# Whole batches first, mixed tiles last, opening masks on TensorE and a new opening order, in an attention and feed-forward kernel

## The chip, the cores and the metric

The kernel runs on one core of one Trainium2 chip. The metric is the device time of one launch in microseconds (us); lower is better.

A profile is one execution. Its span is about 1.7 us shorter than the device time of the same run. Engines: PE is TensorE's matmuls and PEld its weight loads, DVE is VectorE, ACT is ScalarE, POOL is GpSimd, SP is SyncE, which here issues all DMAs.

## The reference

Eight batches of 576 tokens, 8 heads of 64. Each token attends to itself and the 63 tokens before it in its batch; then every token goes through a gated feed-forward block.

```python
def _attn_ref(q, k, v):
    B, H, S, D = q.shape                  # 8, 8, 576, 64
    window = 64
    scores = np.matmul(q, k.transpose(0, 1, 3, 2)) / np.sqrt(D)
    rel = np.arange(S)[:, None] - np.arange(S)[None, :]
    scores = np.where((rel >= 0) & (rel < window), scores, -1e9)
    attn = softmax(scores)
    return np.matmul(attn, v)

def _moe_ref(x, w_gate, w_val, w_out):    # x: 4608 x 512, d_ff 1536
    g = x @ w_gate
    return (g * sigmoid(g) * (x @ w_val)) @ w_out
```

## The kernel before

Tokens are cut into 36 groups of 128, four groups to a feed-forward tile of 512. A batch has 576 = 4.5 x 128 tokens, so every second batch boundary falls in the middle of a group. `load` cuts its DMA there, and one of three masks is chosen for the group. Names: `load(n)` brings keys or queries of 256 tokens (0.52 MB), `load_vg(g)` the values of one group (0.26 MB), `weights(s, i)` a 512 x 256 tile of the gate (0) or value (1) weights (0.52 MB); `turn2` transposes on TensorE, `turn1` through DMA; `step(t, m)` is one of 12 feed-forward steps of a tile (8 matmuls of 512 columns and a tanh), `finish` its VectorE half; `project` is the output matmul; `warm(n)` is n filler matmuls on zeros.

```python
def keys_before(n):                      # last 64 keys of the tile before
    if n:
        dve.tensor_copy(kT[n % KR][:, :, 0:64], kT[(n - 1) % KR][:, :, 256:320])

def weigh(g):                            # exp on ScalarE, mask on VectorE
    E = Es[g % ER]
    mk = masks[0]
    for b in range(2):
        if (2 * g + b) % 9 == 0:
            mk = masks[1 + b]
    for a, x in enumerate(sps.pop(g)):
        e = E[:, a:H:2]
        act.activation(e, x[:], AF.Exp, scale=0.125)
        dve.tensor_mul(e, e, mk[:].unsqueeze(1).to_broadcast([P, 4, 2, 64]))

# the opening, a hand-set order (cut: every "..." leaves lines out)
load(0, k, "k_f"); load(0, q, "q_f")
...
warm(4); scores(0); cast_v(0, (pool, act, dve)); cast_k(1, "k_f", pool)
load(1, q, "q_f"); scores(1); load_vg(2); load(2, k, "k_f"); ...
load(2, q, "q_f") ... load(3, k, "k_f") ... load(3, q, "q_f") ... load_vg(4)
norm(2); products(3); norm(3); cast_k(3, "k_f", pool); weigh(5); turn_x(1); scores(4)
weights(3, 0); cast_k(3, "q_f", pool); weigh(4) ... weights(3, 1)
warm(2); products(4); norm(4); cast_w(3, 1, dve); scores(6); ... step(0, 7)
...
# the regular loop, two groups a turn (cut)
for w in range(8, NG, 2):
    step(t, 3 * s); finish(); ...; scores(w + 4); scores(w + 5); finish(); ...
    turn1(n + 4, "k_f"); keys_before(n + 4); project(t - 1, s); ...
```

The softmax here doesn't subtract the row's maximum and nothing guards it: scores larger than these inputs give would overflow.

## Time and profile before

The device time was 342.47 us, the median of 3 runs (341.31 to 343.25).

| part of the profiled execution (span 342.5 us) | us | read from |
|---|---|---|
| first feed-forward matmul | 31.2 | timeline of TensorE |
| start of the regular loop | 94.3 | timeline of TensorE |
| loop and tail | 248.2 | the rest |
| TensorE busy, 40 to 330 us | 99% | sums by stretch |

The page of before. Each digit is the busy share, in tenths, of one fortieth of the span (8.6 us); PEclk is the clock granted to TensorE, in tenths.

```profile
span 342.5 us, 7053 instructions
...
PE   7677999999999999999999999999999999999996
...
DVE  3869887998577676767676867676777766655520
...
PEclk9968999999999999999999999999999999999999
DMA  8999999997988798979988888898988420200012
...
PE 89%; DMA 4%; DVE 2%; ACT 1%; SPq 1%; issue 1%; ACTq 0%
```

From the fifth slice on TensorE is full, at full clock. Only the first four slices can be shortened; there DMA is 80 to 90% busy or more, VectorE 60 to 90% from the second slice on, and the clock falls. The sums by stretch, with columns PE, PEld, DVE, ACT, POOL (busy us and instructions), clock, DMA share and GB/s:

```profile
10.00:20.00 10.00, 7.11 (x106) 3.99 (x103) 8.46 (x22) 6.99 (x12) 2.38 (x3) 0.89 1.26 227
20.00:30.00 10.00, 6.58 (x111) 4.90 (x113) 7.77 (x21) 7.36 (x13) 6.52 (x8) 0.77 1.11 273
30.00:40.00 10.00, 8.96 (x103) 4.67 (x105) 8.91 (x19) 6.72 (x12) 6.92 (x9) 0.83 1.05 298
```

The chain of waits in the opening (followed back from the last instruction, at each step to what released it), with start and length in us:

```profile
12.90 7.79 DMA q_f<-in_q_dram
...
25.76 2.59 DVE E L191 x4
...
30.95 0.34 PE s_ps L176 x16
31.29 1.65 PE g_ps L269 x4
32.93 1.28 PE v_ps L269 x3
```

It runs through a load of queries that lands at 20.7 us, then through four mask products on VectorE, then into the first step (g_ps), whose matmuls take 0.41 us each: that is the half clock. In the loop they take 0.216 us.

The timeline of TensorE, with start, length, line, operation, shapes and count, gives the first step and the first of the loop:

```profile
31.22 1.72 PE L269 MATMUL g_ps<-xT,wg 128*128 128x512 bf16 x4
...
94.27 1.03 PE L269 MATMUL g_ps<-xT,wg 128*128 128x512 bf16 x4
```

### The profile page before, as it was taken

Reading aid. Unit: us, or ns where it says so; the run is one execution under the profiler, and the core shown is the slowest. Engines: PE = TensorE matmul, PEld = TensorE weight load, DVE = VectorE, ACT = ScalarE, POOL = GpSimd, SP = SyncE. Lnnn points to the kernel's source line nnn. Section 1 sums busy time; section 2 is a strip of 40 time slices with the busy share of each in tenths; the row PEclk is TensorE's granted clock in tenths of the full one; section 3 lists DMA queues with packets and bytes.
Section 4 is the critical chain, followed back from the end, with each engine's and each line's share of the span. In section 5 each row is a group of like instructions: output and inputs, shape, how many; then the busy total and the mean of one; then the engine's idle time right before and its main releaser. Section 6 shows DMA issues by size and latency. Waiting matters only on the chain.

```text
span 342.5 us, 7053 instructions
## 1 busy us (share of the span) xinstructions
PE 327.1 (95%) x2636; PEld 160.9 (47%) x2677; DVE 237.3 (69%) x496; ACT 150.4 (44%) x260; POOL 103.1 (30%) x143
## 2 busy tenths in 40 slices
PE   7677999999999999999999999999999999999996
PEld 3443545455544444444444444444444445444444
DVE  3869887998577676767676867676777766655520
ACT  4756746854362525252525252525343434323222
POOL 2245734552153333332433333333333220000000
PEclk9968999999999999999999999999999999999999
DMA  8999999997988798979988888898988420200012
GB/s 201 236 244 293 322 198 256 352 246 133 181 160 180 167 174 170 171 174 159 186 158 186 155 186 152 190 162 178 179 170 176 110 71 33 62 33 31 31 63 92
DMA packets 148994, 56.70 MB, mean 166 GB/s; under 512 B 122080, under 2 KB 142944, under 8 KB 148960
## 3 DMA queue, kind: packets, MB, share of 16 engines
q1 hardware_dynamic: 148960, 56.25, 77.1%
q8 instruction: 21, 0.34, 0.5%
q14 instruction: 13, 0.11, 0.1%
HBM read 37.75 MB, written 9.44 MB: 138 GB/s over the span
## 4 chain that ended last, share of the span: by engine, by line
PE 89%; DMA 4%; DVE 2%; ACT 1%; SPq 1%; issue 1%; ACTq 0%
PE g_ps L269 28%; PE v_ps L269 27%; PE o_ps L288 26%; DMA q_f<-in_q_dram 4%; PE ao_ps L205 3%; PE s_ps L176 3%; PE tp L147 1%; SPq L81 1%; DVE E L191 1%; DMA out_dram<-os__4803 1%; PE xtp L229 0%; DVE ve L162 0%; ACT q_fb L107 0%; SPq L101 0%; ACT kT L107 0%
## 5 line engine op out<-in xcount | busy, mean ns | idle before, releaser
L280 DVE SCALAR_TENSOR_TENSOR sg<-th,g_ps 128x512 f32<-128x512 f32 (+2 forms) x110 | 74.0, 673 | 56.2 <-ACT th L274 55.9
L269 PE MATMUL g_ps<-xT,wg 128*128 128x512 bf16 (+1 forms) x411 | 110.7, 378 | 2.2 <-DVE sg L280 0.5
L269 PE MATMUL v_ps<-xT,wv 128*128 128x512 bf16 (+2 forms) x435 | 111.0, 377 | 0.1
L274 ACT ACTIVATE th<-g_ps 128x512 f32<-128x512 f32 (+2 forms) x110 | 64.8, 590 | 79.4 <-PE g_ps L269 76.6
L288 PE MATMUL o_ps<-wo,hT 128*128 128x512 bf16 (+2 forms) x453 | 98.5, 368 | 0.2
L281 DVE TENSOR_TENSOR hT<-sg,v_ps 128x512 bf16<-128x512 f32 (+2 forms) x110 | 74.5, 677 | 11.6 <-remote 0.4
L269 PEld LDWEIGHTS <-wv 128*128 128x128 bf16 x440 | 43.0, 98 | 51.2 <-issue 0.5
L288 PEld LDWEIGHTS <-hT 128*128 128x128 bf16 x456 | 43.5, 98 | 49.2
L269 PEld LDWEIGHTS <-wg 128*128 128x128 bf16 x440 | 40.1, 98 | 44.4 <-issue 1.1
L190 ACT ACTIVATE E<-s_ps 128x512 bf16<-128x512 f32 x72 | 38.9, 596 | 12.4 <-PE s_ps L176 12.4
L109 POOL CAST q_fb<-q_f 128x1024 bf16<-128x1024 f32 (+1 forms) x17 | 17.1, 1007 | 87.0 <-DMA q_f<-in_q_dram 85.8
L191 DVE TENSOR_TENSOR E<-E,mask 128x512 bf16<-128x512 bf16 x72 | 34.1, 502 | 9.4 <-ACT E L190 8.6
L109 POOL CAST ve<-v_f 64x512 bf16<-64x512 f32 x57 | 35.6, 625 | 5.2 <-DMA v_f<-in_v_dram 1.7
L109 POOL CAST k_fb<-k_f 128x1024 bf16<-128x1024 f32 (+1 forms) x16 | 15.8, 991 | 56.3 <-DMA k_f<-in_k_dram 45.5
L216 DVE TENSOR_TENSOR x_b<-ao_ps,r 128x256 bf16<-128x256 f32 x72 | 30.5, 424 | 2.5
L109 POOL CAST vo<-v_f 128x512 bf16<-128x512 f32 x30 | 18.9, 631 | 15.1 <-DMA v_f<-in_v_dram 14.8
L205 PE MATMUL ao_ps<-ve,E 128*64 128x65 bf16 x288 | 14.2, 200 | 2.7 <-DVE qT L109 1.6
L205 PEld LDWEIGHTS <-E 128*64 128x64 bf16 x576 | 11.7, 114 | 10.7 <-issue 7.8
L205 PE MATMUL ao_ps<-vo,E 128*64 128x65 bf16 x288 | 14.2, 200 | 0.0
L176 PEld LDWEIGHTS <-kT 64*128 64x128 bf16 x576 | 10.1, 96 | 8.4 <-issue 6.6
L176 PE MATMUL s_ps<-qT,kT 64*128 64x64 bf16 x576 | 12.4, 193 | 1.2 <-DVE qT L109 0.7
L215 DVE RECIPROCAL r<-ao_ps 128x4 f32<-128x4 f32 x72 | 12.4, 172 | 0.6 <-PE ao_ps L205 0.5
(83 smaller groups left out, 130.9 us busy)
## 6 DMA issues: line engine op xcount, KB each, us to landing
v_f<-in_v_dram SPq DMA_DIRECT2D x32, 256.0 KB, 4.4
q_f<-in_q_dram SPq DMA_DIRECT2D x22, 256.0 KB, 4.4
k_f<-in_k_dram SPq DMA_DIRECT2D x22, 256.0 KB, 4.1
w_f<-in_moe_w_gate_dram SPq DMA_DIRECT2D x6, 512.0 KB, 6.7
w_f<-in_moe_w_val_dram SPq DMA_DIRECT2D x6, 512.0 KB, 7.0
wo_f<-in_moe_w_out_dram SPq DMA_DIRECT2D x6, 512.0 KB, 7.8
k_f<-in_k_dram SPq DMA_DIRECT2D x4, 512.0 KB, 6.6
q_f<-in_q_dram SPq DMA_DIRECT2D x4, 512.0 KB, 7.2
```

What stands on the lines that cost most here:

```text
L109: eng.tensor_copy(y, x)
L176: nc.tensor.matmul(ps[a][:, p, b], kT[g // 2 % KR][y, p, o:o + P], qT[g // 2 % QR][y, p, o:o + 64], tile_position=(64 * a, 0),)
L190: act.activation(e, x[:], AF.Exp, scale=0.125)
L191: dve.tensor_mul(e, e, mk[:].unsqueeze(1).to_broadcast([P, 4, 2, 64]))
L205: nc.tensor.matmul(o_ps[64 * b:64 * b + 64, i, :], Es[g % ER][:, y, b], z[g % VR][:, y, :], tile_position=(0, 64 * b),)
L215: dve.reciprocal(r[:], o_ps[:, :, D])
L216: dve.tensor_mul(xb[g][:, 256 * h:256 * h + 256].rearrange("r (y d) -> r y d", y=4), o_ps[:, :, 0:D], r[:].unsqueeze(2).to_broadcast([P, 4 ...
L269: nc.tensor.matmul(ps[:, 0:n], w[:, c, P * m:P * m + P], xT[t][:, c, c0:c0 + n], start=(c == 0), stop=(c == 3),)
L274: act.activation(th[:, 0:n], g_ps[:, 0:n], AF.Tanh, scale=0.5)
L280: dve.scalar_tensor_tensor(sg[:, 0:n], th[:, 0:n], 1.0, g_ps[:, 0:n], ALU.add, ALU.mult)
L281: dve.tensor_mul(hT[t][:, m, c0:c0 + n], sg[:, 0:n], v_ps[:, 0:n])
L288: nc.tensor.matmul(o_ps[:, a:b], hT[t][:, c, P * s:P * s + P], wo[:, c, a:b], start=(c == 0), stop=(c == 11),)
```

## The change

The first 512 tokens of a batch become four whole groups, and the last 64 of two batches share a mixed group (four mixed groups in all, the 29th, 30th, 35th and 36th of the order). No early load is cut at a batch's end. The last keys and values of each batch are kept aside (`kL`, `vL`) until its mixed group comes. Six opening groups (0 and 2 to 6) get their mask from TensorE: after each score matmul a second one adds -1e30 where the mask is zero, and their two VectorE products fall away. The opening is a new hand-set order.

```diff
+    ORDER = [(b, i) for b in range(7) for i in range(4)] + [(0, None), (2, None)]
+    ORDER += [(7, i) for i in range(4)] + [(4, None), (6, None)]
 ...
     def keys_before(n):
-        if n:
-            dve.tensor_copy(kT[n % KR][:, :, 0:64], kT[(n - 1) % KR][:, :, 256:320])
+        b, i = ORDER[2 * n - 1]
+        x = kT[(n - 1) % KR][:, :, 256:320]
+        if i == 3:
+            dve.tensor_copy(kL[:, :, b, 0:64], x)
+        elif i == 1:
+            dve.tensor_copy(kT[n % KR][:, :, 0:64], x)
+
+    def keys_last(n):
+        b, i = ORDER[2 * n]
+        if i is None:
+            dve.tensor_copy(kL[:, :, b:b + 4, 64:P], kT[n % KR]...)   # cut
 ...
-    def scores(g):
+    def scores(g, masked=False):
 ...
+                if masked:
+                    for a in range(2):
+                        y = slice(64 * a, 64 * a + 64)
+                        m = minus[1 if ORDER[g][1] == 0 and b == 0 else 0]
+                        nc.tensor.matmul(
+                            ps[a][:, p, b], m[y], identb[y, y], tile_position=(64 * a, 0),
+                            start=False, stop=True,
+                        )
 ...  (weigh: the mask product only where not masked)
# opening: new order (cut)
+    load(0, q, "q_f")
+    load(0, k, "k_f")
+    cast_k(0, "q_f", (act, dve))
+    load(1, k, "k_f")
+    load_vg(0)
+    cast_k(0, "k_f", (act, pool))
+    load_vg(1)
 ...
+    cast_v(1, (dve, None, None))
+    weigh(1)
+    load(2, q, "q_f")
+    weigh(0)
+    warm(6)
+    products(0)
+    load_vg(2)
+    load_vg(3)
+    weights(5, 0)
+    load_vg(4)
 ...
+    weights(5, 1)
+    load_vg(5)
+    turn2(2, "q_f", act)
+    load(3, k, "k_f")
 ...
+    products(4)
+    cast_w(5, 1, pool)
+    cast_v(5, pool)
+    weigh(5)
+    cast_w(5, 0, dve)
+    step(0, 10, 0, 256)
 ...
# loop and end
             keys_before(n + 4)
+            keys_last(n + 4)
-    for s in range(3):
+    for s in (2, 3, 0):
         project(8, s)
```

More of the change, by code (lines that the diff above doesn't have):

```diff
@@ L32 @@
     NG = NTOK // P
-    NB = NTOK // 256
+    ORDER = [(b, i) for b in range(7) for i in range(4)] + [(0, None), (2, None)]
+    ORDER += [(7, i) for i in range(4)] + [(4, None), (6, None)]
     VW = 65
     KR, VR, ER, QR = 3, 5, 3, 3
+    NEG = -1e30
     ctx.enter_context(tc.manual_schedule())
@@ L58 @@
     ve = [cst.tile([P, H, VW], BF16, name=f"ve{i}") for i in range(VR)]
+    kL = cst.tile([P, 4, 8, P], BF16, name="kL")
+    vL = cst.tile([P, 8, H, VW], BF16, name="vL")
     Es = [cst.tile([P, H, 2, 64], BF16, name=f"E{i}") for i in range(ER)]
-    masks = [cst.tile([P, 2, 64], BF16, name=f"mask{i}") for i in range(3)]
+    masks = [cst.tile([P, 2, 64], BF16, name=f"mask{i}") for i in range(2)]
+    minus = [cst.tile([P, P], BF16, name=f"minus{i}") for i in range(2)]
     identb = cst.tile([P, P], BF16, name="identb")
@@ L67, with tokens @@
     staged = {}
-    def segments(lo, n, step):
-        o = 0
-        while o < n:
-            b, s = divmod(lo + o, S)
-            m = min(n - o, S - s)
-            yield o // step, m // step, b, s, m
-            o += m
+    def tokens(g):
+        b, i = ORDER[g]
+        if i is None:
+            return (slice(0, 64), b, 512), (slice(64, P), b + 1, 512)
+        return ((slice(0, P), b, P * i),)
     def load(n, src, nm):
         x_f = stage.tile([P, H, 2, D], FP32, name=nm, tag=nm)
-        for r, m, b, s, t in segments(256 * n, 256, 2):
-            sp.dma_start(
-                x_f[r:r + m].rearrange("r h c d -> r h (c d)"),
-                src[b, :, s:s + t, :].rearrange("h (r c) d -> r h (c d)", c=2),
-            )
+        ((_, b, s),) = tokens(2 * n)
+        sp.dma_start(
+            x_f[:].rearrange("r h c d -> r h (c d)"),
+            src[b, :, s:s + 256, :].rearrange("h (r c) d -> r h (c d)", c=2),
+        )
         staged[nm, n] = x_f[:].rearrange("r h c d -> r c h d")
@@ L90, in load1 @@
         for i in range(2):
-            for r, m, b, s, t in segments(256 * n + P * i, P, 1):
-                sp.dma_start(x_f[r:r + m, i], src[b, :, s:s + t, :].rearrange("h r d -> r h d"))
+            for y, b, s in tokens(2 * n + i):
+                m = y.stop - y.start
+                sp.dma_start(x_f[y, i], src[b, :, s:s + m, :].rearrange("h r d -> r h d"))
         staged[nm, n] = x_f[:]
@@ L98, in load_vg @@
             staged["v_f", g // 2] = stage.tile([P, 2, H, D], FP32, name="v_f", tag="v_f")[:]
-        x_f = staged["v_f", g // 2]
-        for r, m, b, s, t in segments(P * g, P, 1):
-            sp.dma_start(x_f[r:r + m, g % 2], v[b, :, s:s + t, :].rearrange("h r d -> r h d"))
+        for y, b, s in tokens(g):
+            m = y.stop - y.start
+            sp.dma_start(
+                staged["v_f", g // 2][y, g % 2],
+                v[b, :, s:s + m, :].rearrange("h r d -> r h d"))
     words = {}
@@ L122, in keys_before @@
     def keys_before(n):
-        if n:
-            dve.tensor_copy(kT[n % KR][:, :, 0:64], kT[(n - 1) % KR][:, :, 256:320])
+        b, i = ORDER[2 * n - 1]
[6 more added lines that the diff above has]
+        b, i = ORDER[2 * n]
+        if i is None:
+            dve.tensor_copy(
+                kL[:, :, b:b + 4, 64:P],
+                kT[n % KR][:, :, 64:320].rearrange("r p (b x) -> r p b x", b=4))
     def turn1(n, nm):
@@ L153, in cast_v @@
     def cast_v(g, engs):
+        engs = engs if isinstance(engs, tuple) else (engs,) * 3
         x = staged["v_f", g // 2][:, g % 2]
         lo, hi = slice(0, 64), slice(64, P)
-        engs = engs if isinstance(engs, tuple) else (engs,) * 3
+        b, i = ORDER[g]
         z = vo[g % VR]
-        copy(engs[0], z[:, :, 0:D], x)
-        for e, a, b in ((engs[1], ve[g % VR][hi], lo), (engs[2], ve[(g + 1) % VR][lo], hi)):
+        if i is None:
+            to = (vL[hi, b], lo), (vL[hi, b + 1], hi)
+        else:
+            copy(engs[0], z[:, :, 0:D], x)
+            to = (ve[g % VR][hi], lo), (vL[lo, b] if i == 3 else ve[(g + 1) % VR][lo], hi)
+        for e, (y, a) in zip(engs[1:], to):
             if e is None:
-                dve.tensor_copy(a, z[b])
+                dve.tensor_copy(y[:, :, 0:D], z[a][:, :, 0:D])
             else:
-                copy(e, a[:, :, 0:D], x[b])
+                copy(e, y[:, :, 0:D], x[a])
     sps = {}
-    def scores(g):
+    def scores(g, masked=False):
         ps = [ps_a.tile([P, 4, 2, 64], FP32, name="s_ps", tag="a") for _ in range(2)]
@@ L175, in scores @@
                     y = slice(64 * a, 64 * a + 64)
+                    keys = kT[g // 2 % KR][y, p, o:o + P]
+                    if ORDER[g][1] is None:
+                        keys = kL[y, p, ORDER[g][0] + b, :]
                     nc.tensor.matmul(
-                        ps[a][:, p, b], kT[g // 2 % KR][y, p, o:o + P],
-                        qT[g // 2 % QR][y, p, o:o + 64], tile_position=(64 * a, 0),
-                    )
-        sps[g] = ps
+                        ps[a][:, p, b], keys, qT[g // 2 % QR][y, p, o:o + 64],
+                        tile_position=(64 * a, 0), start=True, stop=not masked,
+                    )
+                if masked:
[5 more added lines that the diff above has]
+                            start=False, stop=True,
+                        )
+        sps[g] = ps, masked
     def weigh(g):
         E = Es[g % ER]
-        mk = masks[0]
-        for b in range(2):
-            if (2 * g + b) % 9 == 0:
-                mk = masks[1 + b]
-        for a, x in enumerate(sps.pop(g)):
+        mk = masks[1 if ORDER[g][1] == 0 else 0]
+        ps, masked = sps.pop(g)
+        for a, x in enumerate(ps):
             e = E[:, a:H:2]
             act.activation(e, x[:], AF.Exp, scale=0.125)
-            dve.tensor_mul(e, e, mk[:].unsqueeze(1).to_broadcast([P, 4, 2, 64]))
+            if not masked:
+                dve.tensor_mul(e, e, mk[:].unsqueeze(1).to_broadcast([P, 4, 2, 64]))
     xT = {}
@@ L199, in products @@
         xps[g] = []
+        c, i = ORDER[g]
+        vs = (ve[g % VR], vo[g % VR]) if i is not None else (vL[:, c], vL[:, c + 1])
         for h in range(2):
@@ L203, in products @@
                 y = 4 * h + i
-                for b, z in enumerate((ve, vo)):
+                for b, z in enumerate(vs):
                     nc.tensor.matmul(
-                        o_ps[64 * b:64 * b + 64, i, :], Es[g % ER][:, y, b], z[g % VR][:, y, :],
+                        o_ps[64 * b:64 * b + 64, i, :], Es[g % ER][:, y, b], z[:, y, :],
                         tile_position=(0, 64 * b),
@@ L283, in project @@
     def project(t, s, parts=((0, DM),)):
-        n0 = 512 * t + P * s
         for a, b in parts:
@@ L293, in project @@
             act.activation(os_[:, a:b], o_ps[:, a:b], AF.Copy, scale=0.5)
-            sp.dma_start(out[n0:n0 + P, a:b], os_[:, a:b])
+            for y, c, n0 in tokens(4 * t + s):
+                n0 += S * c
+                sp.dma_start(out[n0:n0 + y.stop - y.start, a:b], os_[y, a:b])
     def warm(n):
@@ L304, in begin @@
         make_identity(nc, identb[:])
-        for mk in masks:
-            dve.memset(mk[:], 1.0)
+        dve.memset(masks[0][:], 1.0)
+        dve.memset(minus[0][:], 0.0)
         pool.affine_select(
@@ L314, in begin @@
         )
-        dve.memset(kT[0][:, :, 0:64], 0.0)
-        dve.memset(ve[0][0:64], 0.0)
+        for a in range(2):
+            y = minus[0][64 * a:64 * a + 64]
+            pool.affine_select(
+                out=y, in_=y, compare_op=ALU.is_ge, fill=NEG,
+                base=64, pattern=[[-1, P]], channel_multiplier=1,
+            )
+            pool.affine_select(
+                out=y, in_=y, compare_op=ALU.is_ge, fill=NEG,
+                base=-1, pattern=[[1, P]], channel_multiplier=-1,
+            )
@@ L317, in begin @@
+        pool.tensor_copy(minus[1][:, 64:P], minus[0][:, 64:P])
+        pool.memset(minus[1][:, 0:64], NEG)
+        pool.tensor_copy(masks[1][:], masks[0][:])
+        pool.memset(masks[1][0:64, 0, :], 0.0)
+        for i in (0, 2):
+            dve.memset(kT[i][:, :, 0:64], 0.0)
+        for i in (0, 4):
+            dve.memset(ve[i][0:64], 0.0)
         for x in vo + ve:
             dve.memset(x[:, :, D:VW], 1.0)
-        for i in (1, 2):
-            dve.tensor_copy(masks[i][:], masks[0][:])
-            dve.memset(masks[i][0:64, i - 1, :], 0.0)
@@ L323 @@
     begin()
+    load(0, q, "q_f")
     load(0, k, "k_f")
-    load(0, q, "q_f")
-    cast_k(0, "k_f", (dve, act))
-    cast_k(0, "q_f", (act, pool))
+    cast_k(0, "q_f", (act, dve))
[3 more added lines that the diff above has]
+    load_vg(1)
     warm(11)
-    turn2(0, "k_f", act)
-    load_vg(0)
-    load(1, k, "k_f")
+    turn2(0, "q_f", (act, dve))
+    warm(4)
+    turn2(0, "k_f", (act, dve))
+    cast_k(1, "k_f", (dve, act))
     warm(3)
-    turn2(0, "q_f", dve)
@@ L334 @@
-    warm(4)
-    scores(0)
-    cast_v(0, (pool, act, dve))
-    cast_k(1, "k_f", pool)
-    load(1, q, "q_f")
-    scores(1)
-    load_vg(2)
-    load(2, k, "k_f")
-    keys_before(1)
-    weigh(0)
-    cast_k(1, "q_f", dve)
-    weigh(1)
-    warm(2)
-    turn2(1, "k_f", act)
-    warm(2)
-    turn2(1, "q_f", (dve, act))
-    load_vg(1)
-    load(2, q, "q_f")
-    products(0)
-    norm(0)
-    scores(3)
-    cast_k(2, "k_f", (dve, pool))
-    weigh(3)
-    warm(1)
-    turn_x(0)
-    scores(2)
@@ L360 @@
-    cast_v(1, (pool, None, None))
-    weigh(2)
-    load_vg(3)
-    turn2(2, "k_f", act)
-    load(3, k, "k_f")
-    cast_k(2, "q_f", (act, pool))
-    cast_v(2, (pool, dve, act))
-    cast_v(3, (act, pool, pool))
-    warm(2)
-    products(1)
-    norm(1)
-    keys_before(2)
-    warm(4)
-    turn2(2, "q_f", (dve, act))
+    scores(1)
+    load(1, q, "q_f")
+    cast_v(0, (dve, pool, pool))
+    scores(0, True)
+    cast_k(1, "q_f", pool)
+    load(2, k, "k_f")
+    cast_v(1, (dve, None, None))
@@ new lines @@
+    weigh(1)
[7 more added lines that the diff above has]
+    load_vg(4)
+    norm(0)
+    keys_before(1)
+    turn2(1, "k_f", (act, dve))
+    warm(4)
+    turn_x(0)
+    turn2(1, "q_f", (act, dve))
+    products(1)
+    warm(1)
+    scores(2, True)
+    cast_k(2, "k_f", pool)
+    norm(1)
+    cast_k(2, "q_f", dve)
+    weigh(2)
+    warm(1)
+    scores(3, True)
+    weigh(3)
+    weights(5, 1)
+    load_vg(5)
+    turn2(2, "q_f", act)
@@ L374 @@
+    load(3, k, "k_f")
+    cast_v(2, (dve, pool, pool))
+    keys_before(2)
+    turn2(2, "k_f", dve)
+    turn_x(1)
+    warm(2)
     products(2)
     load(3, q, "q_f")
+    norm(2)
+    cast_v(3, (act, pool, pool))
     warm(1)
-    scores(5)
-    load_vg(4)
-    norm(2)
+    scores(4, True)
+    weights(0, 0)
+    weigh(4)
     products(3)
     norm(3)
-    cast_k(3, "k_f", pool)
-    weigh(5)
-    turn_x(1)
-    scores(4)
-    weights(3, 0)
-    cast_k(3, "q_f", pool)
-    weigh(4)
-    turn_x(2)
@@ L390 @@
-    cast_v(4, (pool, None, None))
-    cast_w(3, 0, pool)
-    turn2(3, "k_f", act)
-    turn_x(3)
-    keys_before(3)
-    warm(1)
-    turn2(3, "q_f", (act, dve))
-    weights(3, 1)
-    warm(2)
-    products(4)
-    norm(4)
-    cast_w(3, 1, dve)
-    scores(6)
-    load_vg(5)
-    weigh(6)
-    weights(2, 0)
-    step(0, 7)
-    cast_v(5, (act, pool, pool))
-    scores(7)
-    finish()
-    weights(2, 1)
-    weigh(7)
-    cast_w(2, 0, act)
-    cast_w(2, 1, pool)
-    load_vg(6)
-    products(5)
@@ L416 @@
-    load_vg(7)
-    step(0, 6)
-    turn_x(4)
-    norm(5)
-    cast_v(6, (act, pool, pool))
-    finish()
-    step(0, 5)
-    turn_x(5)
-    finish()
-    weights(1, 0)
-    cast_v(7, (pool, pool, act))
-    weights(1, 1)
-    cast_w(1, 0, pool)
-    products(6)
-    step(0, 4)
-    weights(5, 0)
-    weights(5, 1)
-    products(7)
-    cast_w(1, 1, pool)
-    cast_w(5, 0, pool)
-    step(1, 7, 0, 256)
-    norm(6)
-    weights(4, 1)
+    cast_v(4, (act, pool, pool))
+    warm(1)
+    turn_x(2)
@@ new lines @@
+    warm(2)
+    turn_x(3)
+    weights(0, 1)
+    scores(5, True)
+    products(4)
+    cast_w(5, 1, pool)
+    cast_v(5, pool)
+    weigh(5)
+    cast_w(5, 0, dve)
+    step(0, 10, 0, 256)
+    norm(4)
+    weights(4, 0)
+    step(0, 10, 384, 128)
+    turn_x(4)
+    products(5)
+    load_vg(6)
+    finish()
+    keys_before(3)
+    cast_k(3, "k_f", (act, pool))
+    weights(4, 1)
+    norm(5)
+    finish()
+    step(0, 11)
+    cast_k(3, "q_f", (dve, act))
+    load_vg(7)
+    turn_x(5)
+    turn2(3, "k_f", (dve, act))
@@ L439 @@
+    turn2(3, "q_f", (act, dve))
+    load(4, k, "k_f")
+    cast_w(0, 0, pool)
+    finish()
+    step(1, 11, 0, 256)
+    cast_w(0, 1, act)
+    scores(6, True)
     load(4, q, "q_f")
     finish()
-    turn_x(6)
-    weights(4, 0)
-    load(4, k, "k_f")
-    load(5, q, "q_f")
-    weights_o(1)
-    load_vg(8)
-    step(0, 3)
-    finish()
-    cast_w(5, 1, pool)
-    norm(7)
-    step(0, 2)
+    load_vg(8)
+    scores(7)
+    step(0, 0)
+    weigh(6)
+    step(1, 0, 0, 256)
+    cast_w(4, 0, pool)
@@ L452 @@
     finish()
     finish()
-    turn_x(7)
-    step(0, 10)
-    load_vg(9)
+    weigh(7)
+    cast_w(4, 1, act)
+    cast_v(6, pool)
+    step(0, 1)
+    cast_v(7, (act, pool, pool))
+    products(6)
+    step(0, 8)
+    norm(6)
+    cast_k(4, "k_f", (act, pool))
+    products(7)
+    turn_x(6)
+    finish()
+    norm(7)
+    weights(3, 0)
+    step(0, 9)
+    cast_k(4, "q_f", (act, pool))
+    cast_w(3, 0, pool)
+    weights(1, 0)
+    finish()
+    weights(3, 1)
+    weights(1, 1)
+    keys_before(4)
@@ L457 @@
+    load_vg(9)
+    finish()
+    turn_x(7)
+    cast_w(3, 1, pool)
+    turn2(4, "k_f", (dve, act))
+    turn2(4, "q_f", act)
+    step(1, 8)
+    finish()
+    step(1, 1)
+    weights(2, 0)
+    load(5, q, "q_f")
+    cast_w(1, 0, pool)
+    finish()
+    scores(8)
+    cast_w(1, 1, pool)
+    scores(9)
+    weigh(8)
+    weights_o(4)
+    load(5, k, "k_f")
     step(1, 10)
     finish()
-    cast_k(4, "q_f", pool)
-    step(0, 11)
-    load(5, k, "k_f")
-    cast_w(4, 1, pool)
-    cast_k(4, "k_f", pool)
@@ L464 @@
-    cast_w(4, 0, act)
-    finish()
-    weights(0, 0)
-    load_vg(10)
-    keys_before(4)
-    weights(0, 1)
-    finish()
-    weights_o(0)
-    step(1, 2)
-    finish()
-    step(1, 9)
-    finish()
-    turn2(4, "q_f", (act, dve))
-    step(0, 9)
-    turn2(4, "k_f", act)
-    casts_o(1, pool)
+    cast_w(2, 0, pool)
+    step(0, 6)
+    keys_before(5)
+    weights(2, 1)
+    finish()
     step(1, 6)
     finish()
+    step(0, 2)
+    weights_o(5)
+    cast_k(5, "q_f", pool)
+    finish()
@@ new lines @@
+    weights_o(1)
+    weigh(9)
+    step(0, 7)
+    cast_v(8, act)
+    step(1, 3)
+    finish()
+    cast_k(5, "k_f", (act, pool))
+    step(1, 9)
+    cast_v(9, (dve, pool, pool))
+    finish()
+    cast_w(2, 1, pool)
+    turn2(5, "q_f", act)
+    step(0, 3)
+    weights_o(2)
+    load_vg(10)
+    weights_o(0)
+    finish()
+    casts_o(1, pool)
+    finish()
+    step(0, 10, 256, 128)
+    products(9)
+    casts_o(4, pool)
+    products(8)
+    step(0, 4)
+    norm(9)
+    casts_o(5, pool)
@@ L482 @@
+    finish()
+    finish()
+    turn2(5, "k_f", act)
+    cast_v(10, pool)
+    load_vg(11)
+    step(1, 2)
+    norm(8)
     finish()
     weights_o(3)
-    step(1, 7, 256, 128)
-    finish()
-    cast_k(5, "q_f", pool)
-    scores(9)
-    scores(8)
-    cast_v(8, (act, pool, pool))
-    weigh(9)
-    cast_w(0, 0, pool)
-    weights_o(2)
-    weights_o(5)
-    step(1, 11)
-    keys_before(5)
-    cast_k(5, "k_f", act)
-    step(0, 8)
-    cast_v(9, (pool, dve, act))
-    finish()
-    finish()
@@ L501 @@
-    weights_o(4)
-    cast_w(0, 1, pool)
-    load_vg(11)
-    weigh(8)
-    step(1, 3)
-    turn2(5, "q_f", act)
-    step(1, 8)
-    products(8)
-    finish()
-    products(9)
-    finish()
-    norm(8)
-    step(0, 0)
-    casts_o(0, pool)
-    finish()
-    step(1, 1)
-    turn2(5, "k_f", act)
-    casts_o(3, pool)
-    norm(9)
-    load(6, k, "k_f")
-    turn_x(8)
-    load(6, q, "q_f")
-    step(0, 1)
+    step(0, 5)
+    load1(6, k, "k_f")
+    casts_o(0, pool)
+    load_vg(12)
     finish()
@@ L525 @@
     scores(10)
-    cast_v(10, pool)
+    load(7, k, "k_f")
     scores(11)
-    finish()
-    weigh(10)
-    load1(7, k, "k_f")
-    casts_o(5, pool)
-    casts_o(2, pool)
-    step(1, 0)
-    weigh(11)
-    casts_o(4, pool)
-    project(0, 1)
-    load_vg(12)
-    cast_v(11, (dve, None, None))
-    step(1, 4)
-    products(10)
-    cast_k(6, "q_f", pool)
-    finish()
-    cast_k(6, "k_f", (act, pool))
-    products(11)
-    turn_x1(9)
-    step(1, 7, 384, 128)
-    norm(10)
-    project(0, 0)
@@ L549 @@
-    norm(11)
-    finish()
-    load1(7, q, "q_f")
-    load_vg(14)
-    turn2(6, "k_f", dve)
-    load1(8, k, "k_f")
-    load_vg(13)
-    project(0, 3)
-    step(1, 5)
-    keys_before(6)
+    casts_o(2, pool)
+    casts_o(3, dve)
+    weigh(11)
+    turn_x1(8)
+    keys_before(6)
+    weigh(10)
+    cast_k(6, "k_f", pool)
+    step(1, 7)
+    step(1, 11, 256, 256)
+    finish()
+    turn_x(9)
+    project(0, 3)
+    cast_v(11, (pool, dve, act))
+    load1(6, q, "q_f")
+    turn1(6, "k_f")
+    load1(7, q, "q_f")
@@ L559 @@
+    finish()
+    cast_k(6, "q_f", (act, pool))
+    turn1(6, "q_f")
+    step(1, 5)
+    products(11)
+    norm(11)
+    products(10)
+    cast_k(7, "k_f", (dve, pool))
+    step(1, 0, 256, 256)
+    project(0, 0)
+    norm(10)
+    cast_v(12, (pool, act, act))
     turn_x(10)
-    keys_before(7)
-    turn2(6, "q_f", dve)
-    cast_k(7, "k_f", (dve, pool))
-    turn1(7, "k_f")
     turn_x(11)
     finish()
+    project(0, 1)
+    load_vg(13)
+    finish()
     project(0, 2)
-    cast_v(12, (dve, act, act))
+    load_vg(14)
@@ L570 @@
+    keys_before(7)
+    step(1, 4)
+    turn2(7, "k_f", act)
+    load1(8, k, "k_f")
+    dve.memset(vL[:, :, :, D:VW], 1.0)
     for w in range(8, NG, 2):
@@ L574 @@
         finish()
-        if n + 3 < NB:
+        if n + 3 < NG // 2:
             cast_k(n + 3, "q_f", pool)
@@ L587 @@
         finish()
-        if n + 3 < NB:
+        if n + 3 < NG // 2:
             turn1(n + 3, "q_f")
@@ L592 @@
             load_vg(w + 7)
-        if n + 4 < NB:
+        if n + 4 < NG // 2:
             load1(n + 4, q, "q_f")
@@ L606 @@
                 turn_x1(g)
-        if n + 4 < NB:
+        if n + 4 < NG // 2:
             cast_k(n + 4, "k_f", pool)
@@ L613 @@
         finish()
-        if n + 4 < NB:
+        if n + 4 < NG // 2:
             turn1(n + 4, "k_f")
             keys_before(n + 4)
+            keys_last(n + 4)
         project(t - 1, s)
-        if n + 5 < NB:
+        if n + 5 < NG // 2:
             load1(n + 5, k, "k_f")
@@ L623 @@
     finish()
-    for s in range(3):
+    for s in (2, 3, 0):
         project(8, s)
-    project(8, 3, ((0, 256), (256, 384), (384, DM)))
+    project(8, 1, ((0, 256), (256, 384), (384, DM)))
 _INS = ['q', 'k', 'v', 'moe_w_gate', 'moe_w_val', 'moe_w_out']
```

## The prediction

> **What bounds it now.** The chain of waits gives TensorE 89% of the 342.5 us, DMA 4%. By stretches, TensorE is 99% busy at clock 1.00 from 40 to 330 us. From 10 to 40 us it is busy 6.6 to 9.0 of each 10 us, at clocks 0.89, 0.77, 0.83, and part of that is filler on zeros. By the timeline and chain: first feed-forward step at 31.2 us; opening mixed with steps until the regular loop starts at 94.4 us; loop to 338.2 us (8.5 us per 128 tokens: 7.8 us of 36 512-column matmuls at 0.216 us, 0.7 us of attention); 4.3 us of tail. Only the opening can move.
>
> **What the change does.**
> 1. Loop: same scores, products and steps. Mixed tiles add split DMAs and two 1024-element key copies (about 0.7 us each, from like copies in this trace) on VectorE, which there waits for a key transpose through DMA (2.5 us median) while TensorE has a projection (2.6 us) and a step (1.7 us) to do. I expect under 0.5 us.
> 2. Six opening groups are masked by TensorE: 96 more 64-column matmuls. Sixteen take 0.3 us warm, 0.45 to 0.6 us cold in the timeline: +2 to 3 us of TensorE work, mostly where it idled or ran filler. The Trainium skill ("TensorE: Matmul & The Clock Gate", Part 3) says tiles in different row groups run concurrently; the 0.3 us for 16 agrees.
> 3. They lose 12 mask products on VectorE, 0.50 us each: 6 us. Four of these stand in the chain of before for 2.6 us, just ahead of the first step.
> 4. Less data precedes the first step. Before: eight k/q loads of 0.52 MB, five v loads of 0.26 MB, two weight loads of 0.52 MB, 6.55 MB, landed at about 30 us (218 GB/s). After: six k/q loads, 5.5 MB, so about 25.5 us (an estimate at that rate); with the cast of 1.04 us the first step starts at 26 to 27 us.
> 5. But the second weight pair lands after 7.85 MB, about 34.3 us as in before, plus a cast. So the early start gives about 2.25 steps, then a short hole. At 35.4 us I count 1.75 steps (1.73 us each) more done than before, two x transposes more (0.44 us), and one q/k transpose fewer to do (0.45 us): 3.9 us ahead. I deduct 1 us for stalls and cold clock (same page, Part 1: an idle TensorE falls to half clock; this trace shows 0.43 us instead of 0.216 us for a 512-column matmul there). Later weights arrive before their steps at the recorded rates.
>
> **Sum.** 342.5 - 3.9 + 1 = about 339.4 us, 0.9% faster; 8 in 10: 336.0 to 342.5. Chances: over 2% faster 0.10, within 2% 0.88, over 2% slower 0.02.
>
> **What would show it.** (a) First feed-forward matmul at 25 to 28 us. (b) Loop start at about 91.3 us, and 248 us from there to the end, as before. (c) VectorE's mask products 60 instead of 72; 96 mask matmuls of 1.7 to 3 us in all. (d) A TensorE wait for a weight cast or DMA between 30 and 36 us. (e) TensorE still 99% busy in the loop.
>
> **What would make it wrong.** If the DMA queue moves data faster in the new order (no split key loads in the opening), the hole of step 5 vanishes and the gain is 5 us or more. If the attention chain of the first groups on Scalar and Vector engines, not the data, sets the first step, it comes at 29 us or later and little is gained. If the key copies of the mixed tiles hold up VectorE's finishing of steps, the loop lengthens.

## The result, and the profile after

| | before | changed |
|---|---|---|
| device time, median (range), us | 342.86 (341.31 to 343.33), 4 runs | 338.98 (338.53 to 339.13), 4 runs |
| span of the profiled execution, us | 342.5 | 337.3 |
| first feed-forward matmul, us | 31.2 | 24.6 |
| start of the loop, us | 94.3 | 88.4 |
| loop and tail, us | 248.2 | 248.9 |

The ratio of the times is 0.9892, 95% interval 0.9858 to 0.9927: 1.1% faster. Ratios here are the mean time of one kernel's fast runs over that of the other's of the same rounds, so they are not quite the ratio of the medians quoted. A later control (f4 below) gave 0.9871. The two profiled executions differ by 5.2 us, more than the medians' 3.9, because the profiled execution of before was slower than its own median (344.27 us against 342.86). Each profile below is one execution too; f1's, g2's, g4's and h4's are the fastest of their kernels.

The page of the changed kernel:

```profile
span 337.3 us, 7271 instructions
...
PE   8888999999999999999999999999999999999996
...
DVE  4777899896476867676676665866665866655520
...
PEclk9999999999999999999999999999999999999999
DMA  8999999969998989798989897899696420211014
...
PE 86%; DMA 7%; SPq 4%; issue 1%; POOL 1%; ACT 0%; DVE 0%; POOLq 0%; ACTq 0%
```

TensorE has no cold slice left. The sums by stretch say the same: clock 1.00, more work in each, and a little more from DMA.

```profile
10.00:20.00 10.00, 7.80 (x147) 5.26 (x148) 7.81 (x21) 5.99 (x11) 4.58 (x6) 1.00 1.05 247
20.00:30.00 10.00, 8.08 (x166) 5.60 (x168) 7.45 (x23) 7.07 (x15) 6.87 (x10) 1.00 1.09 291
30.00:40.00 10.00, 9.93 (x127) 5.96 (x128) 8.73 (x19) 8.98 (x17) 5.44 (x7) 1.00 1.15 300
```

The chain of waits in the opening has no mask left; it goes from the first value-weight tile's landing at 25.5 us to its cast on GpSimd and, by way of group 5's values behind it in GpSimd's queue, into the steps:

```profile
18.21 7.28 DMA w_f<-in_moe_w_val_dram
...
25.61 1.04 POOL wv L120
...
26.77 0.63 POOL vo L120
...
28.94 0.59 PE g_ps L309 x2
29.53 0.86 PE v_ps L309 x4
```

The timeline of TensorE shows the first step cut in two by that cast (idle time and releaser in brackets), and the first step of the loop:

```profile
24.64 0.61 PE L309 MATMUL g_ps<-xT,wg 128*128 128x256 bf16 x4
26.71 0.61 PE L309 MATMUL v_ps<-xT,wv 128*128 128x256 bf16 x4 [1.45 <-POOL wv L120]
...
88.44 1.03 PE L309 MATMUL g_ps<-xT,wg 128*128 128x512 bf16 x4
```

So in this pair the opening became 5.8 us shorter, and the loop with its tail 0.6 us longer.

### The profile page after: what moved, and what is told of

Same layout as the page of the kernel before. It is cut to its first block, busy times and chain, and to the rows that moved or that the text cites. A ratio compares the mean times of both kernels' runs of the same rounds, so it can differ in the third digit from the quotient of the medians.

```text
span 337.3 us, 7271 instructions
## 1 busy us (share of the span) xinstructions
PE 326.3 (97%) x2743; PEld 162.8 (48%) x2784; DVE 227.1 (67%) x486; ACT 151.0 (45%) x266; POOL 103.1 (31%) x150
## 4 chain that ended last, share of the span: by engine, by line
PE 86%; DMA 7%; SPq 4%; issue 1%; POOL 1%; ACT 0%; DVE 0%; POOLq 0%; ACTq 0%
PE g_ps L309 27%; PE o_ps L327 26%; PE v_ps L309 26%; PE ao_ps L245 3%; PE s_ps L207 2%; DMA w_f<-in_moe_w_val_dram 2%; DMA v_f<-in_v_dram 2%; SPq L110 2%; DMA q_f<-in_q_dram 1%; PE tp L170 1%; SPq L89 1%; DMA kT<-k_fb 1%; DMA out_dram<-os__4939 1%; SPq L101 1%; SPq L284 0%
## 5 line engine op out<-in xcount | busy, mean ns | idle before, releaser
L320 DVE SCALAR_TENSOR_TENSOR sg<-th,g_ps 128x512 f32<-128x512 f32 (+1 forms) x112 | 74.3, 664 | 57.3 <-ACT th L314 56.9
L309 PE MATMUL g_ps<-xT,wg 128*128 128x512 bf16 (+2 forms) x416 | 110.0, 372 | 2.2 <-DVE sg L320 0.5
L314 ACT ACTIVATE th<-g_ps 128x512 f32<-128x512 f32 (+1 forms) x112 | 65.0, 583 | 78.3 <-PE g_ps L309 76.8
L321 DVE TENSOR_TENSOR hT<-sg,v_ps 128x512 bf16<-128x512 f32 (+1 forms) x112 | 74.9, 668 | 13.1 <-PE v_ps L309 1.7
L120 POOL CAST q_fb<-q_f 128x1024 bf16<-128x1024 f32 (+1 forms) x15 | 14.9, 991 | 69.0 <-DMA q_f<-in_q_dram 57.2
L120 POOL CAST ve<-v_f 64x512 bf16<-64x512 f32 x49 | 31.1, 636 | 8.1 <-DMA v_f<-in_v_dram 5.3
L229 DVE TENSOR_TENSOR E<-E,mask 128x512 bf16<-128x512 bf16 x60 | 27.9, 495 | 8.0 <-ACT E L227 7.4
L120 POOL CAST vo<-v_f 128x512 bf16<-128x512 f32 x24 | 15.0, 625 | 5.9 <-DMA v_f<-in_v_dram 5.6
L245 PE MATMUL ao_ps<-ve,E 128*64 128x65 bf16 x256 | 12.5, 196 | 0.4
L245 PE MATMUL ao_ps<-vo,E 128*64 128x65 bf16 x256 | 12.6, 196 | 0.0
L207 PE MATMUL s_ps<-qT,kT 64*128 64x64 bf16 x512 | 12.2, 191 | 0.3 <-ACT qT L118 0.3
```

What stands on the lines that cost most here:

```text
L120: eng.tensor_copy(y, x)
L207: nc.tensor.matmul(ps[a][:, p, b], keys, qT[g // 2 % QR][y, p, o:o + 64], tile_position=(64 * a, 0), start=True, stop=not masked,)
L245: nc.tensor.matmul(o_ps[64 * b:64 * b + 64, i, :], Es[g % ER][:, y, b], z[:, y, :], tile_position=(0, 64 * b),)
L309: nc.tensor.matmul(ps[:, 0:n], w[:, c, P * m:P * m + P], xT[t][:, c, c0:c0 + n], start=(c == 0), stop=(c == 3),)
L314: act.activation(th[:, 0:n], g_ps[:, 0:n], AF.Tanh, scale=0.5)
L320: dve.scalar_tensor_tensor(sg[:, 0:n], th[:, 0:n], 1.0, g_ps[:, 0:n], ALU.add, ALU.mult)
```

## The experiments

Twelve kernels ran, in three sets of four. Each set has one chip and shares 11 runs of before (medians 342.85, 343.09 and 343.16 us). All gave correct results. My theory at the start was that the data set the first step ("data first"); the rivals were the tiling, the masks, and the clock.

### Tiles, order and masks apart: f1 to f4

f1 is the changed kernel's tiles with the opening of before and masks on VectorE:

```diff
-    (opening of the changed kernel)
+    (opening of before, unchanged)
+    dve.memset(vL[:, :, :, D:VW], 1.0)
```

> The new tiles (whole batches, mixed tiles last) with the opening sequence of before and all masks on VectorE. Theory (the new order of loads and work in the opening makes the gain, by bringing the first weight pair earlier): first feed-forward matmul still at 30 to 32 us, time within 1 us of before, 341.5 to 344. Rival (the tiling itself pays, since no key or value load is split at a batch's end): 340 or less.

f2 is f1 with six groups masked by TensorE:

```diff
-    scores(0)
+    scores(0, True)        # likewise groups 2, 3, 4, 5, 6
```

> As f1, with opening groups 0, 2, 3, 4, 5, 6 masked by TensorE. Theory (data first): the second weight tile still lands at about 30 us, so at most 1.2 us faster than f1. Rival (masks: the 2.6 us of mask products in the chain of before are the gain): at least 2.5 us faster than f1, 340 or less.

f3 is the changed kernel with that taken back:

```diff
-    scores(0, True)
+    scores(0)              # likewise groups 2, 3, 4, 5, 6
```

> The changed kernel with its six opening groups masked by VectorE again. Theory (data first): first step still set by the weight tile that lands at 25.5 us, slower than the changed kernel by at most 1.5 us, 340.5 or less. Rival (masks are the gain): slower by 2.5 us or more, 341.5 or more.

f4 is the changed kernel again, as control.

> The changed kernel unchanged, as a control on the same chip: 338.5 to 339.5 us, ratio 0.986 to 0.992.

Median device times, us (before on this chip: 342.85):

| | masks on VectorE | masks on TensorE |
|---|---|---|
| old order | f1: 342.90 (ratio 0.9972, 0.9934 to 1.0010) | f2: 342.26 (0.9968, 0.9935 to 1.0000) |
| new order | f3: 347.02 (1.0111, 1.0079 to 1.0142) | f4: 338.81 (0.9871, 0.9842 to 0.9900) |

The tiling alone gains nothing that the runs resolve: f1's time is as expected, though its first step was not (28.0 us in its profile, expected 30 to 32). Nor do the masks in the old order. The new order alone loses 4 us. Together they gain 4. My expectation for f3, at most 1.5 us slower, was wrong by far: it was 8.2 us slower than f4. "Data first" as I had it falls: data are one limit, and the masks on VectorE are another.

Why the masks alone do nothing is suggested by f2's chain of waits. The second weight pair's value tile lands at 33.8 us and the value half of its step starts at 35.0, about 0.3 us after the four gate matmuls from 33.8 us would end at 0.216 us each:

```profile
24.84 8.92 DMA w_f<-in_moe_w_val_dram
...
33.89 1.04 POOL wv L120
...
34.98 1.04 PE v_ps L309 x4
```

A longer wait for data comes before it, for group 5's values, which GpSimd can only cast once their load is there:

```profile
30.81 1.28 POOL L120 CAST ve<-v_f 64x512 bf16<-64x512 f32 x2 [3.26 <-DMA v_f<-in_v_dram]
...
31.47 0.19 PE L245 MATMUL ao_ps<-ve,E 128*64 128x65 bf16 x1 [1.09 <-POOL ve L120]
```

So with the masks off VectorE the old order does wait for data, about 1.4 us in all. That this is why f2 gains nothing is argued, not shown. f2's profiled execution has its first step at 28.1 us, 3.1 before that of before, and its loop starts 3.1 us earlier (91.2 us), but its loop and tail take 249.6 us instead of 248.2. f1's has its first step at 28.0 us too, but it is the outlier of 339.89 us, so the two cannot be compared.

Why the order alone loses is in f3's timeline:

```profile
11.05 0.69 DVE L120 CAST vo<-v_f 128x512 bf16<-128x512 f32 x1 [0.74 <-DMA v_f<-in_v_dram]
11.77 0.60 DVE L190 COPY ve<-vo 64x512 bf16<-64x512 bf16 x2
12.41 2.27 DVE L229 TENSOR_TENSOR E<-E,mask 128x512 bf16<-128x512 bf16 x4
...
14.40 0.26 PE L245 MATMUL ao_ps<-ve,E 128*64 128x65 bf16 x1 [3.38 <-DVE E L229]
...
32.73 0.61 PE L309 MATMUL g_ps<-xT,wg 128*128 128x256 bf16 x4 [1.92 <-DVE wg L120]
```

The mask products of groups 1 and 0 stand on VectorE behind the cast of group 1's values, which waited for its load until 11.0 us. TensorE waits 3.4 us for them, its clock falls (0.68 on average from 10 to 20 us, against 1.00 in f4), and the first step comes at 32.7 us instead of 24.7. The Trainium skill ("TensorE: Matmul & The Clock Gate", Part 1, "Architectural detail") says that VectorE's queue is strict first-in, first-out; this trace agrees: a cast and two copies that group 0's products don't need went first.

The products are dear in this place. The twelve ahead of the first step (groups 0 to 5) take 2.27, 2.20, 1.18 and 1.15 us in f3's timeline, 6.8 us in all, 0.57 each, where the median of one is 0.42. Group 1's two, 0.8 us, stand there in f4 as well; f3 adds about 6 us. The longest product here, 1.26 us, is three times the median, and a GpSimd cast ran beside it (13.0 to 14.1 us), but no run isolates the cause.

### Is it one wait, or the sum? h1, h2, h4

Three ways to take f3's first wait away. h1 fills it:

```diff
-    warm(6)
+    warm(20)
     products(0)
```

> f3 (new order, masks on VectorE, 347.0 us) with 14 more fillers in its 3.4 us wait ahead of the first products. If the half clock that followed that wait makes most of f3's loss of 8.2 us: mean clock 0.995 or more and 342 or less. If the delayed chain on VectorE makes it: clock up, but still 344 or more.

h2 moves the masks of groups 1 and 0 ahead of group 1's values:

```diff
-    cast_v(1, (dve, None, None))
     weigh(1)
     load(2, q, "q_f")
     weigh(0)
+    cast_v(1, (dve, None, None))
```

> f3 with the mask products of groups 0 and 1 issued on VectorE ahead of group 1's value copies, which wait for a load that lands at 11.0 us. Theory (the masks hurt because VectorE works in order and stood behind that load): the first products start near 12 us instead of 14.7 and at least 3 us of the 8.2 come back, 344 or less. Rival (the 6 us of mask work on VectorE count by their sum): at most 1 us comes back.

h4 masks group 0 alone on TensorE (`scores(0, True)` in f3).

> f3 with group 0 alone masked by TensorE. If the first wait starts the loss: at least 3 of the 8.2 us come back, 344 or less, first products near 11.3 us. If each of the six masks costs its share in the chain: about 1.4 us comes back, 345.6.

| | median us | first products at | first step at |
|---|---|---|---|
| f3 | 347.02 | 14.4 | 32.7 |
| h1 | 346.26 (1.0075, 1.0048 to 1.0101; five fast runs) | | |
| h2 | 346.42 (ratio 1.0069, 1.0039 to 1.0099) | 12.2 | 30.1 |
| h4 | 345.72 (1.0058, 1.0021 to 1.0095) | 11.1 | 29.8 |
| f4 | 338.81 | 11.1 | 24.7 |

h1's sixth run, the profiled one, took 355.84 us at a mean clock of 0.945. It is over 1.5% above the fastest run of its kernel and is left out, so h1 has no profile to read.

The first products came as early as I expected in h2 and h4, and only 0.6 and 1.3 us came back. Filler gave back 0.8 us. These runs were on another chip than f3; by the ratios to before it is 1.4, 1.8 and 1.2 us, and the intervals overlap f3's. So the first wait is not most of the loss as far as these runs tell, though h4's interval is too wide to exclude 3 us; in h4 the rival's number, 345.6, was met. h1 did not settle the clock: its fast runs have 0.985 to 0.995 where the test asked for 0.995 or more (f3 has 0.979 to 0.990). But g2 below, at 0.988 to 0.990, is only 1.8 us slower than f4, so a clock like that need not cost 8 us. h4's first step shows what remains:

```profile
29.82 0.61 PE L309 MATMUL g_ps<-xT,wg 128*128 128x256 bf16 x4 [1.94 <-DVE wg L120]
```

The cast of the first gate weights stands on VectorE behind group 5's mask, as it did in f3 (1.92 us). No run takes this last wait away alone, for instance by casting these weights on another engine, so its share is not known. What is seen: most of the loss outlives the first wait, and the added products' sum, about 6 us, is of the size of the delay of the first step, 8.0 us. That the delay is this sum, passed on from wait to wait through an in-order engine, is argued from the timeline, not shown by a run. h4's runs spread from 343.05 (the profiled one) to 347.32, so its share is rough.

### Are data a limit in the new order? g1

```diff
     load_vg(2)
     load_vg(3)
+    load(3, k, "k_f")
+    load(3, q, "q_f")
     weights(5, 0)
     load_vg(4)
```
(and both loads taken out of their later places)

> The changed kernel with the fourth key and query loads (1.05 MB) moved ahead of the first weight tile, so that 6.55 MB must again land before the first weight pair, as in before. Theory (data set the first step): the first feed-forward value matmul starts at 30 us or later instead of 26.7, and the time rises by 3 to 4.5 us, to 341.8 to 343.3. Rival (the masks on TensorE and the clock are all of it, data have slack): at most 1 us slower, 339.8 or less.

343.90 us, ratio 1.0022 (1.0001 to 1.0043): 5 us slower than the changed kernel's 338.8 to 339.0, the whole gain and a little more. Its masks are still on TensorE. In the timeline:

```profile
27.34 1.29 POOL L120 CAST ve<-v_f 64x512 bf16<-64x512 f32 x2 [5.45 <-DMA v_f<-in_v_dram]
...
28.47 0.22 PE L245 MATMUL ao_ps<-ve,E 128*64 128x65 bf16 x1 [4.15 <-ACT xT L270]
...
30.14 1.06 PE L309 MATMUL v_ps<-xT,wv 128*128 128x256 bf16 x4
```

The value matmul of the first step starts at 30.1 us instead of 26.7, as expected. The first wait that binds is one place earlier than I thought: group 4's values, which follow the weight tile in the queue. (The name ScalarE at TensorE's wait misleads: ScalarE's copy of xT came after its own cast of the same values, which waited 4.42 us for that load.) The time rose a little more than the expected 3 to 4.5 us; the clock in this trace is 0.94 and 0.89 in the stretches from 20 and 30 us, and part of it may lie there.

### Is it the clock? g2, g3

g2 takes 18 fillers out of the changed kernel, all those after the first scores:

```diff
-    warm(6)                # likewise warm(4), (1), (1), (2), (1), (1), (2) further on
     products(0)
```

> The changed kernel without its 18 filler matmuls after the first scores. Theory (clock: the opening keeps full clock only because TensorE is never idle for long): mean clock below 0.99 and at least 2 us slower, 340.8 or more. Rival (the real work of the new order, with 96 mask matmuls, keeps the clock by itself, or the clock does not matter while data set the pace): within 0.7 us of the changed kernel.

g3 gives 11 more to the kernel of before:

```diff
-    warm(2)
+    warm(5)
     products(1)
     norm(1)
     keys_before(2)
-    warm(4)
+    warm(10)
 ...
-    warm(2)
+    warm(4)
     products(4)
```

> The kernel of before with 11 more fillers, in the two long waits around its second products and ahead of its fifth. Theory (clock is a main part of what before loses): mean clock 0.995 or more and at least 1.5 us faster than before, 341.4 or less. Rival (data and attention chain set the pace of the old order): within 0.7 us of before.

g2: 340.58 us (ratio 0.9927, 0.9902 to 0.9952), mean clock 0.988 to 0.990; about 1.8 us worse than f4's 338.81. Both are just short of what the theory named (below 0.99, at least 2 us), and far from the rival's 0.7 us. g3: clock 0.994 to 1.000 where before had 0.985 to 0.995, and the time is the same as before: 343.25 us, ratio 1.0002 (0.9980 to 1.0024). So before's half clock is a sign of its waits rather than their cause: with the clock mended, the first step of g3's profiled execution still stood at 30.9 us. In the new order the fillers are worth 1.8 us.

g2's sums by stretch show how little idle time is enough:

```profile
11.00:12.00 1.00, 0.71 (x17) 0.53 (x18) 0.80 (x2) 0.46 (x1) 0.58 (x1) 0.83 1.16 295
12.00:13.00 1.00, 1.00 (x10) 0.73 (x8) 0.96 (x4) 0.39 (x1) 0.00 (x0) 0.50 1.16 290
...
18.00:19.00 1.00, 1.00 (x32) 0.91 (x27) 0.32 (x2) 0.92 (x3) 0.11 (x1) 0.76 0.68 123
```

The clock drops to one half at about 11.7 us and comes back at about 18.5, though TensorE's longest wait in this part was 1.2 us. In this execution (339.50 us) that cost the opening nothing: the first step comes at 24.7 us and the loop at 88.3, both as in f4's profile. Where g2's slower runs lose their time is not traced.

### The loop's one wait, and an attempt at a better opening: g4, h3

In the changed kernel's loop, VectorE and TensorE each wait for something new. The list of waits says (us in total, times, longest):

```profile
DVE kL L145 <- DMA kT<-k_fb: 7.1, 2, 3.8
...
PE g_ps L309 <- DVE sg L320: 0.5, 1, 0.5
```

The key copy of a mixed pair waits for a transpose through DMA issued just before it, and once the `finish` behind it comes late for TensorE (0.47 us, at 261 us). g4 issues the copy two steps later:

```diff
-            keys_last(n + 4)         # end of the turn
 ...
         finish()
+        if n + 3 < NG // 2:
+            keys_last(n + 3)         # in the next turn, after its second finish
         if w + 5 < NG:
             weigh(w + 4)
```

> The changed kernel with the two key copies of the mixed tiles issued on VectorE about two steps later. Theory (the one wait of TensorE in the regular loop, 0.5 us at 261 us, is VectorE held up by the key transpose): that wait is gone, time 0.5 us less than the changed kernel, about 338.3. Rival (the 0.5 us comes back in another wait or was noise): no change.

Both waits are gone from its trace. The time is 338.68 us, ratio 0.9869 (0.9848 to 0.9889), against f4's 338.81 and 0.9871: a difference of 0.13 us, which the runs do not resolve.

h3 is g4 with the first value-weight tile ahead of group 4's values, to shorten the 1.45 us wait in the first step, and the first steps ahead of group 4's products:

```diff
     weights(5, 0)
+    weights(5, 1)
     load_vg(4)
 ...
     scores(5, True)
-    products(4)
     cast_w(5, 1, pool)
 ...
     step(0, 10, 384, 128)
+    cast_v(4, (act, pool, pool))
     finish()
     step(0, 11)
+    finish()
+    products(4)
```

> g4 with the first value-weight tile loaded ahead of group 4's values, and the first one and three quarter steps placed before group 4's products. Theory (data set the first step, TensorE waits 1.0 to 1.45 us there for the weight cast): the wait shrinks and 0.5 to 1.2 us are gained over g4, 337.5 to 338.2. Rival (the wait moves to group 4's values or the next weights): within 0.3 us of g4.

341.98 us (ratio 0.9959, 0.9934 to 0.9985): 3.3 us worse than g4, and worse than the rival allowed. The wait did go: the first value matmul starts at 25.0 us. But group 4's values and everything behind them came late, and TensorE starved just after (waits of the whole execution, of which 1.8 and 0.9 us lie between 24 and 45 us, then the stretch from 30 us):

```profile
PE xtp L269 <- DVE x_b L256: 2.6, 6, 0.6
PE tp L170 <- DVE q_fb L120: 1.9, 2, 0.9
```

```profile
30.00:40.00 10.00, 7.87 (x109) 5.46 (x104) 6.26 (x14) 6.61 (x13) 5.14 (x7) 0.83 1.11 293
```

TensorE is busy 7.9 of these 10 us at clock 0.83, where the changed kernel has 9.9 at 1.00. I changed the load order and the work order at once, so the shares of the two are open. No experiment is clearly better than the changed kernel.

## Why the prediction was right

The time, 338.98 us, lies 0.4 us from the forecast 339.4, and the change stayed within 2%. Point by point:

- **Only the opening can move (right).** The loop and tail took 248.2 and 248.9 us.
- **Step 1, the loop loses under 0.5 us (about right).** One wait of 0.47 us came, from the mechanism named: VectorE held up by the key transpose (3.3 and 3.8 us). The copies took 0.43 us each, not 0.7. g4 took the wait away.
- **Step 2, 96 mask matmuls cost 2 to 3 us (somewhat less).** The pairs follow each other at 0.03 us, so eight more pairs a group and six groups make 1.4 us. A mask pair sits between two score pairs without a gap; the skill's row-group concurrency (Part 3) holds here too: 64 columns at the loop's rate of 0.216 us for 512 would take 0.027 us for each of the two, one after the other (an estimate).
- **Step 3, masks leave VectorE (right in kind, not given its due).** 60 products instead of 72. The text lists the gain but gives it no term in the sum, because it took data to be the only limit. f3 shows it worth 8.2 us in the new order, f2 about nothing in the old one.
- **Step 4, less data ahead of the first step (right).** Estimated landing of the first pair 25.5 us, measured 25.5; first step at 26 to 27 us, measured 24.6 for its gate half (just below the 25 to 28 us of (a)) and 26.7 for its value half. g1 put the data back and lost 5 us.
- **Step 5, a hole of TensorE between 30 and 36 us and 1 us off for stalls and clock (wrong).** There was no such wait; the wait of 1.45 us came earlier, in the first step. The second pair's gate tile was cast from 31.6 us and its value tile from 33.1, where I had set the value tile at 34.3 us plus a cast, and TensorE did not stand idle for either. DMA was a little faster (311 and 249 GB/s in the fourth and third slice, against 293 and 244), and the clock stayed at 1.00; that faster data would close the hole is the first risk that the prediction names. By 35.2 us 3.25 steps were done against 1 in before, a lead of 2.25 instead of my 1.75.
- **The sum (right in total, partly by luck).** The opening of the profiled pair gained 5.8 us where I wrote about 3. The undeserved deduction (1 us) and the half step counted too few (0.9 us) make most of the difference; the rest I did not track. But the profiled execution of before, from which I took all its times, was 1.4 us slower than its median, so the pair overstates the gain: the medians differ by 3.9 us. I had started the sum from the median.

The mechanism as the runs leave it: in the new order both the masks on TensorE (8.2 us, f3) and the later loads (5 us, g1) are needed, and the fillers are worth 1.8 us (g2). Moving the masks alone gave nothing that the runs resolve (f2), and the new order alone lost 4 us (f3). My reading is that before stood under two limits at once, the data ahead of the first weight pairs and a chain of masks through VectorE, so that either held when the other was lifted; that is argued from the waits of f2 and f3, not shown.

What stays open: why f1, the old order on new tiles, ran once at 339.89 us with clock 0.999 and otherwise at 341.46 to 343.33 with 0.989 to 0.995, though g3 shows that a better clock alone does not speed up before; and how f3's 8.2 us divide between mask time, queue order and clock. In f1's fast execution the loads were early: 306 GB/s from 30 to 40 us against f2's 276, and the cast of the second value-weight tile began at 32.5 us instead of 33.9. That fits a limit by data, but it is one execution, and it came near the changed kernel with the old order and with masks on VectorE.

## What to carry to other kernels

When two limits end at nearly the same time, an ablation of one shows nothing; cross the parts in a two-by-two before calling either worthless. Count a start-up as bytes that must land before the first useful matmul, and as the serial work of each in-order engine up to it; the later of the two decides, and it changes with every edit. Before moving one load forward in a tuned order, follow what it pushes back: in h3, where the work order changed too, 1.2 us saved at the first value matmul came with over 3 us more in total.

## What the Trainium skill lacked or had wrong

- "TensorE: Matmul & The Clock Gate", "HAM oscillation": the rule against idle gaps of more than about 3.4 us is not enough, and the page's next section, which says that frequent micro-idles can do it too, gives no length for them. In g2 the clock fell to 0.50 from 12 to 18 us although TensorE's longest wait there was 1.2 us; f4, which differs only in having the fillers, stayed at 1.00. In f3 the clock fell at about 13.6 us by its sums of single microseconds, some 2.6 us into a wait of 3.4 (an estimate).
- "TensorE: Matmul & The Clock Gate", "Back-to-back issue gap": it gives about 131 ns for each 512-column matmul in a sustained stream with weight loads and says that 216 ns over-counts. Here 12 such matmuls, each with its own weight load, take 2.59 us on the chain, 216 ns each, through the whole loop. The measurement decides.
- "TensorE: Matmul & The Clock Gate", Part 4: it gives about 275 ns for one 128 x 128 transpose in a kernel's context, and says that the full clock does not engage for transposes. Here one takes 219 to 233 ns on average (before), and because they overlap eight in a row take 0.62 us from first start to last end; at half clock eight take 1.04 us, so they do go faster at the full clock.
